# Block 0 of a fused attention and two-MLP kernel: one weight-decoding turn a step, with GpSimd's share and the attention's pieces put elsewhere in the step

## The chip, the cores and the metric

The kernel runs on one core of one Trainium2 chip. Five engines have a queue each and run it strictly in order: TensorE (PE, matmuls), VectorE (DVE), ScalarE (ACT), GpSimd (POOL) and SyncE (SP, which here only starts DMAs). They wait for each other through semaphores. The metric is the device time of one execution in microseconds (us); less is better.

## The reference, cut to what matters

```python
q_s = softmax(q over features)           # q, k, v: 8 batches, 8 heads, 576 rows, 64 features, float32
k_s = softmax(k over the sequence)
x = q_s @ (k_s^T @ v)                    # per batch and head; then (4608 tokens, 512)
h = x @ moe_w_in                         # 512 -> 2048; the weights come as 8-byte floats
x = (h - tanh(h)) @ moe_w_out            # 2048 -> 512
h = x @ moe2_w_in                        # 512 -> 2048
out = (P(h) / (Q(h) + 1e-6)) @ moe2_w_out    # P a cubic, Q = 1 + |b0||h| + |b1|h^2
```

## The kernel before, in words

The 4608 tokens are nine blocks j of 512. In the first MLP a step n treats one slice f = n % 16 of 128 hidden features of block j = n // 16. A float32 operand is split into a rounded high part and the low rest, and each product is three matmuls (`mm3`, lines 80 to 82): so `first_product(f)` is 12 matmuls of 128x512 into `hps`, and `second_product1` of the step two before (LAG1 = 2) is 12 more into `acc`. Between them stand, for every step: `t` = tanh(hps) on ACT (line 983), `hps` = hps - t on DVE (line 986, called sub here), `gh`, the high part, on ACT (line 336), and `gl`, the low part (line 340), on DVE in block 0 and on POOL later. `gh` and `gl` have two buffers, so a new `gh` waits until the second product of two steps before has read the old one.

Steps 0 to 15 are block 0, and only there the weights of the first MLP are still on their way: each 128x512 piece arrives as 8-byte floats (`raw`, 512 KB, three buffers) and is decoded. ACT makes two pieces of the word (`e` line 131, `m` line 133); DVE takes the sign (`and`, line 134), shifts (line 146) and adds (line 147); ACT copies the high part (`wa..h`, `wb..h`, line 154, called high here); DVE or POOL takes the low part (`wa..l`, `wb..l`, line 158, called low). 32 pieces are needed in block 0, seven of which are opened in the prologue. One call of `decode` opens one piece, joins (shift and add) the one opened in the call before, and takes the high and the low part of still older ones. Block 0 has two such calls in a step (one in steps 2 and 6): the first between sub and `gl`, with its low on DVE, the second behind `gl`, with its low on POOL.

Beside that, block 0 prepares the attention of block 1, in pairs of heads p = 0 to 3 that begin every third step: `kv_max` (DVE, lines 456 and 457), `kv_turn` (PE), `kv_top` (DVE, `mc`, line 474), `kv_back` (PE, line 479, needs `mc`), `kv_sub` (DVE, `ke`, line 485), `kv_exp` (ACT, line 495), `kv_mm` (PE) and `kv_norm` (`rs` on DVE, `bd` on ACT, line 527); and for the queries `q_max` (DVE, `qm`), `q_sub` (POOL), `q_exp` (ACT, line 605), `q_sum` (`qs` in three DVE instructions from line 610, then a multiplication on POOL, line 613), `q_turn` and `q_mm` (PE), `q_copy` and `q_out` (ACT, `qh` and four copies to `xr`, line 674). `work[n]` lists what step n does of it; `front` issues the plain entries at the head of the step, `turn` the PE half of the paired ones, and `follow` their second half, behind `gl`.

The order on every engine is the order in which this program is written. From step 16 on there is no decoding of this kind and no part of the change.

Of the kernel before, what the change touches and what calls it, by code (L numbers as in the profile page):

```python
# [18 lines left out]
P = 128  # L19
# [24 lines left out]
def attention_moe_moe2_kernel(ctx, tc, q, k, v, w1, w2, w3, w4, ca, cb, out):  # L44
# [31 lines left out]
    def f32(ap):  # L76
        return ap.bitcast(F32)
# [24 lines left out]
        [(0, "a", 0)] + [x for f in range(-1, KF) for x in ((0, "b", f), (0, "a", f + 2)) if 0 <= x[2] < KF],  # L102
        [(1, w, f + i) for f in range(0, KF, 2) for w in "ab" for i in range(2)],
    ]
    staged, joining, parting = [], [], []

    def staging():
        return rawp.tile([P, 2 * NB], F32, tag="raw", name="raw")
# [14 lines left out]
    def dec_open(t):  # L123


        words = t.bitcast(U32).rearrange("p (n two) -> p n two", two=2)
        e = decp.tile([P, NB], F32, tag="e", name="e", bufs=3)
        m = decp.tile([P, NB], U32, tag="m", name="m", bufs=4)


        ACT.activation(out=e, in_=f32(words[:, :, 1]), func=AF.Copy, scale=2.0**-112)
        halves = m.bitcast(U16).rearrange("p (n two) -> p n two", two=2)
        ACT.activation(out=halves[:, :, 0], in_=words[:, :, 0], func=AF.Copy, scale=2.0**-29)
        DVE.tensor_scalar(  # L134
            out=halves[:, :, 1],
            in0=t.bitcast(U16).rearrange("p (n four) -> p n four", four=4)[:, :, 3],
            scalar1=0x8000,
            scalar2=None,
            op0=ALU.bitwise_and,
        )  # L140
        return e, m
# [18 lines left out]
    def dec_start():  # L160

        old = [joining.pop()] if joining else []
        if staged:
            piece, t = staged.pop(0)
            if wide:
                joining.append((piece, t, *dec_open(t)))
            else:
                old.append((piece, t, None, t))
        return old

    def dec_end(ph, old, low_on_dve):
        if parting and parting[0][2]:
            dec_low(*parting.pop(0)[:2], low_on_dve)
        for x in parting:
            dec_high(*x[:2])
            x[2] = True
        if wide:
            for _, _, e, m in old:
                dec_join(e, m)
        parting.extend([piece, m, False] for piece, _, _, m in old)  # L180
        fetch_w(ph)

    def decode(ph, low_on_dve):
        dec_end(ph, dec_start(), low_on_dve)

    parked = {}
    UNITS = (1, 5, 2, 6, 7, 4, 3)
# [495 lines left out]
    def front(todo):  # L685
        for fn, args in todo:
            if not isinstance(fn, tuple):
                fn(*args)

    def turn(todo):  # L690

        got = []
        for fn, args in todo:
            if isinstance(fn, tuple):
                fn[0](*args)
                got.append(lambda fn=fn, args=args: fn[1](*args))
        return got

    def follow(after):
        for fn in [late for fn in after for late in [fn()] if late]:  # L700
            fn()

# [19 lines left out]
    for j in range(1, NBLK):  # L722
        for p in range(NPAIR):
            if j < B:
                s, at = kv_from[j, p], kv_at[j, p]
                steps = (s - 2, s - 1 - (p == 0), s - (p == 0), s + (p > 0), at) if j == 1 else (s - 3, s - 3, s - 1, s, s, s, at)
                for fn, s in zip(KV if j == 1 else KV_LATER, steps):
                    if fn is not kv_max or (j, p) != (1, 0):
                        put(s, fn, j, p)
            s, at = q_from[j, p], q_at[j, p]  # L730
            steps = (s - 1, s, s + 1, s + 2, at - 2, at) if j == 1 else (s - 1, s, s + 1, s + 2, s + 3, s + 5, at)
            for fn, s in zip(Q if j == 1 else Q_LATER, steps):
                if fn is not q_max or (j, p) != (1, 0):
                    put(s, fn, j, p)
        for p in range(2, NPAIR + 2):
            to, before = (j + p // NPAIR, p % NPAIR), (j + (p - 2) // NPAIR, (p - 2) % NPAIR)
            if to in kv_at:
                put(kv_from[before] + 1, load_k, *to)
                put(kv_at[before] + 1, load_v, *to)
            if to in q_at:  # L740
                put(q_from[before] + 2, load_q, *to)

    with tc.manual_schedule():
# [21 lines left out]
        for s in range(NPAIR + 4):  # L765
            def at(k, *fns):

                return [fn(0, s - k) for fn in fns if 0 <= s - k < NPAIR]

            at(1, kv_turn)  # L770
            at(2, kv_back)
            at(3, kv_mm, q_turn)
            at(4, q_mm)
            at(0, kv_max, q_max, q_sub)
            at(1, q_exp)
            at(1, kv_top)
            at(2, q_sum)
            at(2, kv_sub, kv_exp)
            at(3, kv_sum, q_copy)
            at(3, kv_parts)  # L780
            if s < NPAIR + 3:
                if s >= 2:
                    decode(0, False)
                at(5, q_out)
            else:
                kv_max(1, 0)
                q_max(1, 0)
                at(5, q_out)
                at(4, q_out)
                decode(0, False)  # L790
                decode(0, False)
# [150 lines left out]

        STEPS = NBLK * KF
        PAIRS = STEPS // 2
        due = {}
        last = STEPS - KF
        for n in range(STEPS):
            j, f = n // KF, n % KF
            leave = None
            front(work[n])  # L950
            flush()
            hps = first_product(f)
            if f == KF - 1 and j + 1 < NBLK:
                next_x()
            if n == last:
                ACT.activation(out=absb, in_=coef[:, 4:6], func=AF.Abs)
                DVE.tensor_scalar(out=coef[:, 0:4], in0=coef[:, 0:4], scalar1=-1.0, scalar2=None, op0=ALU.mult)
            if n == last + 10:
                for errand in todo:
                    for _ in errand:  # L960
                        flush()
                flush()
                for pool in (att, bdp, decp, rawp):
                    pool.release()
                outp = ctx.enter_context(tc.tile_pool(name="outp", bufs=4, side="right"))
                rp = ctx.enter_context(tc.tile_pool(name="rp", bufs=2, side="right"))
                xup = ctx.enter_context(tc.tile_pool(name="xup", bufs=1, side="right"))
                units = [xup.tile([P, NB], F32R, tag=f"u{k}", name=f"u{k}") for k in range(12)]
                units += [w[:, c, :] for w in (xh, xl) for c in range(KC)]
# [5 lines left out]
            if n in due:  # L975
# [5 lines left out]
            after = turn(work[n])  # L981
            t = gp.tile([P, NB], F32, tag="t", name="t", bufs=1)
            ACT.activation(out=t, in_=hps, func=AF.Tanh)  # L983

            g = t if j else hps
            DVE.tensor_tensor(out=g, in0=hps, in1=t, op=ALU.subtract)  # L986
            ph_w, turns = None, 0
            if j == 0:
                ph_w, turns = 0, 1 if f in (2, 6) else 2
            gh, gl = split_high(g)  # L990
            due[n + LAG1] = lambda a=(j, f, gh, gl): second_product1(*a)
            if turns:
                decode(ph_w, True)
            split_low(g, gh, gl, POOL if j else DVE)
            follow(after)
            if leave:
                leave()
            if turns > 1:
                decode(ph_w, False)
            if n == KF:  # L1000
                fetch_w(1)
            if n > KF:
                for errand in todo:
                    next(errand, None)
            if n == STEPS - 1:

                ACT.activation(out=ahead, in_=bias_q, func=AF.Abs_reciprocal_sqrt)
# [69 lines left out]
```

## Time and profile before

| | |
|---|---|
| time, three runs | 1654.87 us median (1653.03 to 1655.1) |
| the profiled execution | 1656.78 us, span 1655.0 us |
| PE busy | 1615.7 us, 98% of the span |
| DVE, ACT, POOL busy | 67%, 62%, 63% of the span |
| step 1's sub to step 13's, in block 0 | 79.83 us, 12 steps |

A share over the whole span says little of block 0, which is one sixteenth of it and the only stretch in which DVE is nearly full. Times in rows are microseconds from the span's start, and a row's second number is how long the instruction took. The distance between two starts on one engine is often a little shorter than that, since an instruction begins before the last one has left the engine; the sums go by these distances.

### The profile page before, as it was taken

Reading aid. Unit: us, or ns where it says so; the run is one execution under the profiler, and the core shown is the slowest. Engines: PE = TensorE matmul, PEld = TensorE weight load, DVE = VectorE, ACT = ScalarE, POOL = GpSimd, SP = SyncE. Lnnn points to the kernel's source line nnn. Section 1 sums busy time; section 2 is a strip of 40 time slices with the busy share of each in tenths; the row PEclk is TensorE's granted clock in tenths of the full one; section 3 lists DMA queues with packets and bytes.
Section 4 is the critical chain, followed back from the end, with each engine's and each line's share of the span. In section 5 each row is a group of like instructions: output and inputs, shape, how many; then the busy total and the mean of one; then the engine's idle time right before and its main releaser. Section 6 shows DMA issues by size and latency. Waiting matters only on the chain.

```text
span 1655.0 us, 26931 instructions
## 1 busy us (share of the span) xinstructions
PE 1615.7 (98%) x9400; PEld 1375.3 (83%) x9400; DVE 1109.6 (67%) x1839; ACT 1024.5 (62%) x1821; POOL 1039.2 (63%) x876
## 2 busy tenths in 40 slices
PE   5999999999999999999999999999999999999998
PEld 3777888888888888887888989898999999999996
DVE  7997656575565556351214787778787777878786
ACT  6785554544545455443326777777777777777775
POOL 4223727374554637373435888888888877888775
PEclk9999999999999999999999999999999999999999
DMA  8662766666474756351487575858585757676640
GB/s 233 192 182 80 217 175 191 169 186 190 147 208 118 227 150 202 104 174 56 142 305 284 178 281 193 285 189 295 190 297 199 276 195 265 206 252 217 208 139 26
DMA packets 250729, 323.76 MB, mean 196 GB/s; under 512 B 119008, under 2 KB 185568, under 8 KB 241376
## 3 DMA queue, kind: packets, MB, share of 16 engines
q1 hardware_dynamic: 250592, 322.03, 60.9%
q8 instruction: 74, 1.21, 0.3%
q14 instruction: 63, 0.52, 0.1%
HBM read 249.04 MB, written 72.93 MB: 195 GB/s over the span
## 4 chain that ended last, share of the span: by engine, by line
PE 82%; DVE 7%; DMA 3%; ACT 3%; issue 2%; SPq 1%; POOL 1%; DVEq 0%; ACTq 0%; POOLq 0%
PE acc L80 14%; PE acc L81 14%; PE acc L82 14%; PE z L871 12%; PE y L871 9%; PE hps L80 6%; PE hps L81 6%; PE hps L82 6%; DVE m L147 1%; DVE m L134 1%; PE kvps L515 1%; PE xps L660 1%; DMA xh<-x2d 1%; DVE e L146 1%; DVE xl L322 0%
## 5 line engine op out<-in xcount | busy, mean ns | idle before, releaser
L340 POOL TENSOR_TENSOR gl<-t,gh 128x512 fp32r<-128x512 f32 x128 | 174.1, 1360 | 301.0 <-ACT gh L336 278.1
L928 POOL TENSOR_TENSOR n<-n,r 128x512 f32<-128x512 f32 x144 | 186.6, 1296 | 98.2 <-ACT r L925 93.0
L986 DVE TENSOR_TENSOR t<-hps,t 128x512 f32<-128x512 f32 x128 | 88.1, 688 | 233.4 <-ACT t L983 233.4
L336 ACT CAST gh<-t 128x512 fp32r<-128x512 f32 x128 | 79.8, 623 | 248.0 <-PE acc L82 140.5
L928 POOL TENSOR_TENSOR n<-n,n 128x512 f32<-128x512 f32 x144 | 186.7, 1296 | 36.1 <-ACT n L912 36.1
L928 POOL TENSOR_TENSOR n<-n,h 128x512 f32<-128x512 f32 x144 | 187.2, 1300 | 9.7 <-DMA xl<-x2d 9.6
L983 ACT ACTIVATE t<-hps 128x512 f32<-128x512 f32 x144 | 86.0, 597 | 121.0 <-PE hps L82 85.3
L882 ACT COPY sums<-z 128x256 f32<-128x256 f32 x144 | 53.8, 374 | 135.0 <-PE z L871 135.0
L908 ACT ACTIVATE n<-h,coef 128x512 f32<-128x512 f32 x144 | 116.7, 810 | 0.3 <-POOL n L928 0.3
L938 DVE CAST gh<-a 128x512 fp32r<-128x512 f32 x144 | 99.6, 692 | 16.5 <-PE z L871 0.9
L941 DVE TENSOR_TENSOR gl<-a,gh 128x512 fp32r<-128x512 f32 x144 | 99.7, 692 | 15.2 <-DVE gh L938 0.5
L934 DVE SCALAR_TENSOR_TENSOR a<-a,n 128x512 f32<-128x512 f32 x144 | 100.0, 695 | 14.3 <-POOL n L928 8.5
L917 DVE SCALAR_TENSOR_TENSOR a<-h,absb,a 128x512 f32<-128x512 f32 x144 | 107.6, 747 | 3.0 <-ACT a L902 2.9
L902 ACT ACTIVATE a<-h,coef 128x512 f32<-128x512 f32 x144 | 100.5, 698 | 2.7 <-DVE gl L941 2.7
L931 DVE SCALAR_TENSOR_TENSOR a<-a,r 128x512 f32<-128x512 f32 x144 | 99.4, 690 | 0.8 <-ACT r L925 0.8
L920 ACT ACTIVATE r<-a,bias_q 128x512 f32<-128x512 f32 x144 | 97.3, 676 | 0.0
L925 ACT ACTIVATE r<-r 128x512 f32<-128x512 f32 x144 | 91.2, 634 | 4.6
L905 ACT ACTIVATE h<-h 128x512 f32<-128x512 f32 x144 | 89.3, 620 | 0.9 <-DMA xh<-x2d 0.8
L889 DVE TENSOR_TENSOR h<-y,sums 128x256 f32<-128x256 f32 x72 | 30.6, 425 | 58.6 <-PE y L871 58.6
L893 DVE TENSOR_TENSOR h<-y,top 128x512 f32<-128x512 f32 x72 | 49.7, 691 | 27.4 <-ACT top L882 27.1
L613 POOL TENSOR_TENSOR qe<-qe,qs 128x512 f32<-128x512 f32 x36 | 40.6, 1128 | 38.7 <-DVE qs L612 35.4
L80 PE MATMUL acc<-wb3h,gh 128*128 128x512 f32 x144 | 57.0, 396 | 2.9 <-DVE gh L938 2.9
(296 smaller groups left out, 5114.2 us busy)
## 6 DMA issues: line engine op xcount, KB each, us to landing
u<-x2d SPq DMA_DIRECT2D x78, 256.0 KB, 5.5
raw<-in_moe_w_in_dram SPq DMA_DIRECT2D x32, 512.0 KB, 4.8
raw<-in_moe_w_out_dram SPq DMA_DIRECT2D x32, 512.0 KB, 4.1
x2d<-raw SPq DMA_DIRECT2D x64, 256.0 KB, 3.5
x2d<-xr SPq DMA_DIRECT2D x56, 256.0 KB, 3.8
wa0h<-wa0d SPq DMA_DIRECT2D x9, 1024.0 KB, 5.0
wa1h<-wa2d SPq DMA_DIRECT2D x9, 1024.0 KB, 5.0
wa2h<-wa4d SPq DMA_DIRECT2D x9, 1024.0 KB, 5.2
```

The costliest lines, as they stand in the source:

```text
L80: PE.matmul(o, lhi, rhi, start=start, stop=False)
L81: PE.matmul(o, lhi, rlo, start=False, stop=False)
L82: PE.matmul(o, llo, rhi, start=False, stop=stop)
L340: eng.tensor_tensor(out=gl, in0=g, in1=f32(gh), op=ALU.subtract)
L871: PE.matmul(o, w, x[:, xc], start=m in (1, 5) and c == k == 0, stop=c == 1 and k == 2, skip_group_check=True,)
L902: ACT.activation(out=new(t, "a", ps_a), in_=t["h"], func=AF.Abs, scale=b0)
L908: ACT.activation(out=new(t, "n1"), in_=t["h"], func=AF.Identity, scale=a3, bias=a2)
L917: DVE.scalar_tensor_tensor(out=t["a"], in0=t["h2"], scalar=b1, in1=t["a"], op0=ALU.mult, op1=ALU.add)
L928: return lambda t: POOL.tensor_tensor(out=t[a], in0=t[a], in1=t[b], op=op)
L934: DVE.scalar_tensor_tensor(out=t["a"], in0=t["a"], scalar=2.0, in1=t["n0"], op0=ALU.subtract, op1=ALU.mult)
L938: DVE.tensor_copy(out=t["g"][0], in_=t["a"])
L941: DVE.tensor_tensor(out=t["g"][1], in0=t["a"], in1=f32(t["g"][0]), op=ALU.subtract)
```

## The change

It gives block 0 one turn a step in place of two calls. A step opens two pieces, joins the same two in the same step, and takes the high part of the first of them at its end (`highs(1)`) and of the second at the head of the next step, right behind tanh (`highs(2)`). POOL's low part is issued there too; DVE's low part comes behind `gl`. The plain attention entries named in `BESIDE` move from the head of a step to the place between sub and `gl`; `kv_exp` and `q_exp` (`CLOSING`) move to the step's end; `kv_top` and `kv_sub` (`beside`) run between sub and `gl` of the next step instead of behind `gl` of their own. The prologue joins one piece more and fetches one more. One load of keys is a step later. All 32 pieces and all arithmetic stay.

```diff
+    def opens(n):
+        for _ in range(min(n, len(staged))):
+            piece, t = staged.pop(0)
+            if wide:
+                opened.append((piece, *dec_open(t)))
...
+            fetch_w(0)
+    def joins(n):
+        for _ in range(min(n, len(opened))):
+            piece, e, m = opened.pop(0)
+            if wide:
                 dec_join(e, m)
+            joined.append((piece, m))
+    def highs(n):
+        for _ in range(min(n, len(joined))):
+            dec_high(*joined[0])
+            ready.append(joined.pop(0))
+    def lows(*engines):
+        for eng in engines[:len(ready)]:
+            dec_low(*ready.pop(0), eng is DVE)
...
+    BESIDE = (kv_max, kv_squares, kv_join, kv_sub, q_max, q_sub, q_sum, q_squares)
+    CLOSING = (kv_exp, q_exp)
...
-            front(work[n])
+            front(work[n], () if j else BESIDE + CLOSING)
...
             ACT.activation(out=t, in_=hps, func=AF.Tanh)
             g = t if j else hps
             DVE.tensor_tensor(out=g, in0=hps, in1=t, op=ALU.subtract)
-            ph_w, turns = None, 0
-            if j == 0:
-                ph_w, turns = 0, 1 if f in (2, 6) else 2
+            if not j:
+                highs(2)
+                first = ready[0:1]
+                del ready[0:1]
+                lows(POOL, POOL)
+                follow(beside)
+                only(work[n], BESIDE)
+                if n in due:
+                    due.pop(n)()
+                after = turn(work[n])
+                beside = [x for x in after if x[0] in (kv_top, kv_sub)]
+                after = [x for x in after if x not in beside]
             gh, gl = split_high(g)
             due[n + LAG1] = lambda a=(j, f, gh, gl): second_product1(*a)
-            if turns:
-                decode(ph_w, True)
             split_low(g, gh, gl, POOL if j else DVE)
+            if not j:
+                for x in first:
+                    dec_low(*x, True)
+                opens(2)
+                joins(2)
+                highs(1)
             follow(after)
+            if not j:
+                only(work[n], CLOSING)
             if leave:
                 leave()
-            if turns > 1:
-                decode(ph_w, False)
```

On ACT, at the end of step 2, the kernel before has these rows, from step 2's `gh` to the next tanh (`t`). `m` and `e` open a piece, `wa1h` and `wb0h` are highs, `ke` and `qe` the two exponentials.

```order
L336 CAST gh<-hps 128x512
L131 ACTIVATE e<-raw 128x512
L133 ACTIVATE m<-raw 128x512
L154 CAST wa1h<-m 128x512
L131 ACTIVATE e<-raw 128x512
L133 ACTIVATE m<-raw 128x512
L154 CAST wb0h<-m 128x512
L495 ACTIVATE ke<-ke 128x640
L605 ACTIVATE qe<-qe 128x512
L983 ACTIVATE t<-hps 128x512
```

The changed kernel has, for the same stretch and on to the next step's first rows:

```order
L344 CAST gh<-hps 128x512
L131 ACTIVATE e<-raw 128x512
L133 ACTIVATE m<-raw 128x512
L131 ACTIVATE e<-raw 128x512
L133 ACTIVATE m<-raw 128x512
L154 CAST wa1h<-m 128x512
L503 ACTIVATE ke<-ke 128x640
L613 ACTIVATE qe<-qe 128x512
L1001 ACTIVATE t<-hps 128x512
L154 CAST wb1h<-m 128x512
```

Before, a high copied a piece that had been joined one call earlier; now `wa1h` copies the piece whose `e` and `m` stand three and four rows above it, and the exponentials and the tanh are queued behind it.

On DVE, the kernel before has these rows from step 2's sub to step 3's: `gl` is the low part of g, `wb0l` a decoding low, and `qs` and `mx` are the attention's of step 3's head.

```order
L986 TENSOR_TENSOR hps<-hps,t 128x512
L134 TENSOR_SCALAR m<-raw 128x512
L158 TENSOR_TENSOR wb0l<-m,wb0h 128x512
L146 TENSOR_SCALAR e<-e 128x512
L147 ISA m<-e,m 128x1024
L340 TENSOR_TENSOR gl<-hps,gh 128x512
L610 TENSOR_REDUCE qs<-qe 128x8
L611 TENSOR_SCALAR qs<-qs 128x8
L612 RECIPROCAL qs<-qs 128x8
L456 TENSOR_TENSOR mx<-kt_159 128x256
L457 TENSOR_TENSOR mx<-mx,kt_159 128x128
L986 TENSOR_TENSOR hps<-hps,t 128x512
```

And the changed kernel's step 3, which has the same attention entries, from its sub to its second shift (an add and step 4's sub follow):

```order
L1004 TENSOR_TENSOR hps<-hps,t 128x512
L618 TENSOR_REDUCE qs<-qe 128x8
L619 TENSOR_SCALAR qs<-qs 128x8
L620 RECIPROCAL qs<-qs 128x8
L464 TENSOR_TENSOR mx<-kt_159 128x256
L465 TENSOR_TENSOR mx<-mx,kt_159 128x128
L348 TENSOR_TENSOR gl<-hps,gh 128x512
L158 TENSOR_TENSOR wa1l<-m,wa1h 128x512
L134 TENSOR_SCALAR m<-raw 128x512 x2
L146 TENSOR_SCALAR e<-e 128x512
L147 ISA m<-e,m 128x1024
L146 TENSOR_SCALAR e<-e 128x512
```

The decoding left the place between sub and `gl`, the attention went there, and the whole turn stands behind `gl`.

On DVE at the start of block 0, the kernel before has `mc` (for `kv_back` of step 1) behind step 0's `gl`:

```order
L147 ISA m<-e,m 128x1024
L340 TENSOR_TENSOR gl<-hps,gh 128x512
L474 TENSOR_REDUCE mc<-kvps 128x1
L134 TENSOR_SCALAR m<-raw 128x512
L146 TENSOR_SCALAR e<-e 128x512
```

The changed kernel has it behind step 1's sub, with step 0's whole turn in between:

```order
L348 TENSOR_TENSOR gl<-hps,gh 128x512
L158 TENSOR_TENSOR wb0l<-m,wb0h 128x512
L134 TENSOR_SCALAR m<-raw 128x512 x2
L146 TENSOR_SCALAR e<-e 128x512
L147 ISA m<-e,m 128x1024
L146 TENSOR_SCALAR e<-e 128x512
L147 ISA m<-e,m 128x1024
L1004 TENSOR_TENSOR hps<-hps,t 128x512
L482 TENSOR_REDUCE mc<-kvps 128x1
```

PE's own order is the same in both kernels: first product of the step, second product of two steps before, then the attention's matmuls.

## Rows read from the trace of the kernel before

**Rows 1.** Stretches: us, busy of PE, PEld, DVE, ACT, POOL; clock; DMA share, GB/s.

```profile
47.94:127.77 79.83, 77.88 (x448) 60.86 (x447) 74.74 (x141) 60.94 (x113) 20.52 (x17) 0.99 0.59 178
127.77:148.01 20.24, 16.62 (x76) 12.38 (x74) 15.91 (x29) 11.94 (x25) 4.00 (x4) 0.92 0.16 38
```

**Rows 2.** Instruction groups, DVE, the first of these stretches: busy us, mean ns.

```profile
L134 DVE TENSOR_SCALAR m<-raw 128x512 uint16<-128x512 uint16 x22 | 15.7, 712 | 0.0
L146 DVE TENSOR_SCALAR e<-e 128x512 uint32<-128x512 uint32 x22 | 10.8, 493 | 0.0
```

**Rows 3.** Timeline of DVE, steps 2 and 3: start, duration, instruction.

```profile
54.37 0.70 DVE L986 TENSOR_TENSOR hps<-hps,t 128x512 f32<-128x512 f32 x1
54.98 0.46 DVE L134 TENSOR_SCALAR m<-raw 128x512 uint16<-128x512 uint16 x1
55.32 0.67 DVE L158 TENSOR_TENSOR wb0l<-m,wb0h 128x512 fp32r<-128x512 f32 x1
55.92 0.42 DVE L146 TENSOR_SCALAR e<-e 128x512 uint32<-128x512 uint32 x1
56.37 0.69 DVE L147 CUSTOM_DVE_ANT_0 m<-e,m 128x1024 uint16<-128x1024 uint16 x1
56.98 0.68 DVE L340 TENSOR_TENSOR gl<-hps,gh 128x512 fp32r<-128x512 f32 x1
57.58 0.68 DVE L610 TENSOR_REDUCE qs<-qe 128x8 f32<-128x512 f32 x1
...
58.61 0.37 DVE L456 TENSOR_TENSOR mx<-kt 128x256 f32<-128x256 f32 x1
59.02 1.02 DVE L457 TENSOR_TENSOR mx<-mx,kt 128x128 f32<-128x128 f32 x1
```

**Rows 4.** Timelines of POOL and DVE: instructions beside each other, and one alone.

```profile
58.84 1.05 POOL L613 TENSOR_TENSOR qe<-qe,qs 128x512 f32<-128x512 f32 x1 [6.47 <-DVE qs L612]
...
80.34 0.29 DVE L457 TENSOR_TENSOR mx<-mx,kt 128x128 f32<-128x128 f32 x1
...
51.06 1.31 POOL L158 TENSOR_TENSOR wa1l<-m,wa1h 128x512 fp32r<-128x512 f32 x1 [4.15 <-ACT wa1h L154]
...
51.14 0.81 DVE L485 TENSOR_TENSOR ke<-kt,kvps 128x640 f32<-128x640 f32 x1
```

**Rows 5.** Timeline of ACT: exponentials, tanh and gh of step 2; step 7's copies.

```profile
52.61 0.73 ACT L495 ACTIVATE ke<-ke 128x640 f32<-128x640 f32 x1
53.24 0.61 ACT L605 ACTIVATE qe<-qe 128x512 f32<-128x512 f32 x1
53.77 0.57 ACT L983 ACTIVATE t<-hps 128x512 f32<-128x512 f32 x1
55.16 0.59 ACT L336 CAST gh<-hps 128x512 fp32r<-128x512 f32 x1 [0.82 <-DVE hps L986]
...
87.67 1.52 ACT L674 COPY xr<-xps 64x256 f32<-64x256 f32 x4
89.21 0.32 ACT L527 ACTIVATE bd<-xps,rs 128x64 f32<-128x64 f32 x1
```

**Rows 6.** Timelines of DVE and ACT: an add and its high; a gh and its gl.

```profile
39.23 0.69 DVE L147 CUSTOM_DVE_ANT_0 m<-e,m 128x1024 uint16<-128x1024 uint16 x1
...
39.96 0.62 ACT L154 CAST wb0h<-m 128x512 fp32r<-128x512 f32 x1 [1.49 <-DVE m L147]
...
136.59 0.59 ACT L336 CAST gh<-hps 128x512 fp32r<-128x512 f32 x1 [2.99 <-DVE hps L986]
...
137.21 0.69 DVE L340 TENSOR_TENSOR gl<-hps,gh 128x512 fp32r<-128x512 f32 x1
```

**Rows 7.** Timeline of PE: kv_back of step 1; step 14's second product, and the next.

```profile
45.03 0.32 PE L479 MATMUL kvps<-identity,mc 128*128 128x128 f32 x1 [3.47 <-DVE mc L474]
...
145.27 0.40 PE L80 MATMUL acc<-gh,wb3h 128*128 128x512 f32 x1
...
148.01 0.39 PE L80 MATMUL hps<-xh,wa0h 128*128 128x512 f32 x1
```

More of the change, by code (lines that the diff above doesn't have):

```diff
@@ L104, in attention_moe_moe2_kernel @@
     ]
-    staged, joining, parting = [], [], []
+    staged, opened, joined, ready = [], [], [], []
     def staging():
@@ L158, in dec_low, with decode @@
         (DVE if on_dve else POOL).tensor_tensor(out=lo, in0=f32(m), in1=f32(hi), op=ALU.subtract)
-    def dec_start():
-        old = [joining.pop()] if joining else []
-        if staged:
+    def opens(n):
+        for _ in range(min(n, len(staged))):
             piece, t = staged.pop(0)
             if wide:
-                joining.append((piece, t, *dec_open(t)))
+                opened.append((piece, *dec_open(t)))
             else:
[L168 to L178, printed above, removed]
-                dec_join(e, m)
[L180 to L184, printed above, removed]
+                m = decp.tile([P, NB], U32, tag="m", name="m", bufs=4)
+                POOL.tensor_copy(out=f32(m), in_=t)
+                opened.append((piece, None, m))
+            fetch_w(0)
[3 more added lines that the diff above has]
+            if wide:
+                dec_join(e, m)
+            joined.append((piece, m))
[6 more added lines that the diff above has]
+            dec_low(*ready.pop(0), eng is DVE)
+    def decode():
+        n, r = len(opened), len(ready)
+        opens(1)
+        lows(*[POOL] * r)
+        highs(1)
+        joins(n)
     parked = {}
@@ L683, in attention_moe_moe2_kernel, with front, only @@
     Q_LATER = (q_max, q_sub, q_exp, q_sum, q_squares, q_fetch, (q_mm, q_out))
-    def front(todo):
+    BESIDE = (kv_max, kv_squares, kv_join, kv_sub, q_max, q_sub, q_sum, q_squares)
+    CLOSING = (kv_exp, q_exp)
+    def front(todo, leave=()):
         for fn, args in todo:
-            if not isinstance(fn, tuple):
+            if not isinstance(fn, tuple) and fn not in leave:
+                fn(*args)
+    def only(todo, these):
+        for fn, args in todo:
+            if fn in these:
                 fn(*args)
@@ L695, in turn @@
                 fn[0](*args)
-                got.append(lambda fn=fn, args=args: fn[1](*args))
+                got.append((fn[1], args))
         return got
     def follow(after):
-        for fn in [late for fn in after for late in [fn()] if late]:
-            fn()
+        for fn, args in after:
+            fn(*args)
     work = {s: [] for s in range(NBLK * KF)}
@@ L737, in attention_moe_moe2_kernel @@
             if to in kv_at:
-                put(kv_from[before] + 1, load_k, *to)
+                put(kv_from[before] + (2 if before[0] == 1 else 1), load_k, *to)
                 put(kv_at[before] + 1, load_v, *to)
@@ L782, in attention_moe_moe2_kernel @@
                 if s >= 2:
-                    decode(0, False)
+                    decode()
                 at(5, q_out)
@@ L789, in attention_moe_moe2_kernel @@
                 at(4, q_out)
-                decode(0, False)
-                decode(0, False)
+                decode()
+                decode()
+                joins(1)
+                fetch_w(0)
             if s in (4, 5):
@@ L944, in attention_moe_moe2_kernel @@
         PAIRS = STEPS // 2
-        due = {}
+        due, beside = {}, []
         last = STEPS - KF
@@ L974, in attention_moe_moe2_kernel @@
                     load_unit(0, u)
-            if n in due:
+            if j and n in due:
                 leave = due.pop(n)()
@@ L980, in attention_moe_moe2_kernel @@
                 ring(f // 4 - 1)
-            after = turn(work[n])
+            after = turn(work[n]) if j else []
             t = gp.tile([P, NB], F32, tag="t", name="t", bufs=1)
@@ L986, in attention_moe_moe2_kernel @@
             DVE.tensor_tensor(out=g, in0=hps, in1=t, op=ALU.subtract)
-            ph_w, turns = None, 0
-            if j == 0:
-                ph_w, turns = 0, 1 if f in (2, 6) else 2
+            if not j:
[10 more added lines that the diff above has]
+                after = [x for x in after if x not in beside]
             gh, gl = split_high(g)
             due[n + LAG1] = lambda a=(j, f, gh, gl): second_product1(*a)
-            if turns:
-                decode(ph_w, True)
             split_low(g, gh, gl, POOL if j else DVE)
+            if not j:
[3 more added lines that the diff above has]
+                joins(2)
+                highs(1)
             follow(after)
+            if not j:
+                only(work[n], CLOSING)
             if leave:
                 leave()
-            if turns > 1:
-                decode(ph_w, False)
             if n == KF:
```

## The prediction

> **What bounds the kernel now.** I read the shares of the engines first (PE 98% of the span), so anything that delays PE costs its full length and anything else costs nothing. Then the waits of PE inside block 0, since the change touches nothing else, and the busy times of the engines in two stretches: step 1's sub to step 13's, and from there to the second first product of block 1, at 148.01 us [rows 1, 7]. In the first, 79.83 us for twelve steps (6.65 us each), PE is busy for 77.88 and DVE for 74.74: both are nearly full, and only 1.95 us of PE is idle. In the second, 20.24 us, PE is busy for 16.62 and its granted clock is 0.92. Ahead of both lies one wait of 3.47 us, when `kv_back` of step 1 stands on PE for `mc` from DVE [rows 7]. So a shorter DVE step could win little more than PE's idle time, while a step that becomes longer than 6.65 us by DVE or ACT is paid almost in full.
>
> Second, I read DVE's and ACT's timelines for what a step is made of. DVE's starts follow each other by 0.61 us (sub), 0.34 (and), 0.60 (low), 0.45 (shift), 0.61 (add) and 0.60 (gl) [rows 3]. Part of DVE's time is stretching: the and takes 0.712 us on average and 0.46 where nothing is beside it, the shift 0.493 and 0.42 [rows 2, 3], in all 22 x 0.25 + 22 x 0.07 = 7.1 us. The last row of the DVE timeline shows what stretches: the second `kv_max` instruction took 1.02 us beside a POOL multiplication that ran from 58.84 to 59.89, and 0.29 alone [rows 3, 4].
>
> **The change: removed.** The stretching of ands and shifts. POOL's low starts when its high is done, now right behind tanh, and lies beside sub, attention and `gl`; the ands come later. `ke` took 0.81 us beside a POOL low of 1.31 and so wasn't held until that ended [rows 4]; the ones that read PSUM or one tensor I cost at nothing. So up to 7.1 us of DVE's work goes.
>
> **Added: a circle of waits.** This decides. Before, a high on ACT copied a piece joined a call earlier, so tanh of the next step didn't wait for this step's DVE work. Now the last high of a step waits for the first add of the same step, and tanh of the next step is queued behind it on ACT; sub waits for tanh, `gh` for sub, `gl` for `gh`, and the low, the ands, the shift and that add stand behind `gl` on DVE. A step can't be shorter than once around: tanh to sub 0.60, sub to gh 0.79 [rows 3, 5], gh to gl 0.62 [rows 6], gl 0.60, low 0.60, two ands 0.68, shift 0.45 [rows 3], add to high 0.73 [rows 6], high to tanh 0.53 (as exponential to tanh) [rows 5]: **5.60 us**, in which DVE stands idle for 0.80 between sub and gl (0.79 + 0.62 - 0.61). The rest of the second piece's work hides beside high and tanh. Twelve steps: 67.2, less 0.3 as step 12 has one piece only: 66.9.
>
> **Added: what lies on the circle besides.** *On ACT, between high and tanh*, nothing hides the closing entries: `kv_exp` 0.63 in steps 2, 6, 9, 12; `q_exp` 0.53 in step 2; `q_copy` about 0.53 in 5, 8, 11, 12; in steps 7 and 10 four copies, `bd` and `q_exp`, 1.54 + 0.22 + 0.53 = 2.29 [rows 5]; in step 4 `bd` waits for `rs`, which DVE takes behind its second add, about 0.8 + 0.22 + 0.53 = 1.56. Sum: 2.5 + 0.5 + 2.1 + 4.6 + 1.6 = **11.3 us**. *On DVE, between sub and gl*, the attention is free only up to the 0.80. `qs` takes 1.03 (57.58 to 58.61), the maxima 0.41 + 0.29, `ke` 0.8, and `qm` and `mc` I take as 0.6 and 0.4 by the like rows [rows 3, 4]. Over 0.80: steps 2 (ke, qm) 0.6, 3 (qs, maxima) 0.9, 5 and 8 (mc, qs, qm) 1.2 each, 6 and 9 (ke, maxima) 0.7 each, 11 (mc, qs) 0.6: **5.8 us** with rounding.
>
> **Added: two-input instructions beside POOL.** POOL's low now runs from about 1.2 to 2.5 us behind tanh, and `q_sub` or `q_sum`'s product follows it at once (1.05) [rows 4]. The maxima stand in that place: the first waits for the low (0.5), the second for POOL's next (1.0). Steps 6 and 9: 1.55 each; step 3: 1.3: **4.4 us**. Bounds: nothing, or this. I take it whole because the row of 1.02 us is the same instruction. DVE's own low also reads two SBUF tensors and meets `q_sub` or the product in steps 1 (1.1), 3 (0.5) and 11 (0.7): **2.3 us**. No row shows this pair; bounds nothing and 2.3, and I take the upper, by its likeness to that row. The Trainium skill (SBUF — State Buffer, Who interferes with whom) says that a VectorE instruction with two SBUF inputs contends with a GpSimd instruction that reads SBUF, and that the later one blocks fully: by it the 2.3 is paid, without it the sum would be 2.3 less. The trace agrees for the maxima (1.02 against 0.29); for the low no row tells.
>
> **Moved: `mc` and `kv_back`.** `mc` of step 1 now stands behind step 0's whole turn and step 1's tanh and sub. The prologue's extra join puts sub of step 0 off by 1.06, to 42.4; once around from there (0.79 + 0.62 + 0.60 + 0.60 + 0.68 + 0.45 + 0.73 + 0.53 + 0.60, and 0.4 for a low behind POOL's) is 6.0, so sub of step 1 comes at 48.4 (before 47.94): **+0.5**. PE's wait for `mc` grows from 3.47 to about 8 us (45.03 to 49.4). It is not on the circle, but the product behind it is late and may run at a lower clock, and `gh` of step 2 waits for the second product of step 0 behind that: **+0.8** (bounds 0 and 2). The loads issued by SP keep three raw buffers and are needed a whole step after their issue; the later load of keys has two steps: nothing. Should these covers fail, a step waits by what a load is late.
>
> **Moved: the end of the turns.** Pieces are all opened by step 12, before by step 13. From tanh of step 13 on PE has only its own work: `kv_mm` (about 1.3 until its end), six halves of a step at 2.74 (145.27 to 148.01 for twelve matmuls [rows 7]) and 1.0 for `q_mm`: 18.8, or 18.2 from sub, against 20.24 [rows 1]: **-2.0**.
>
> **Sum.** 66.9 + 11.3 + 5.8 + 4.4 + 2.3 + 0.8 = 91.5 for the twelve steps, against 79.83: +11.7; with +0.5 and -2.0: **+10.2 us**. The profiled execution took 1656.78 (its span 1655.0), so 1667.0 by its own time; it lies 1.9 above the median of the runs, and the forecast for a median is 1654.87 + 10.2 = 1665. From block 1 on nothing changes and PE is full, so nothing is given back.
>
> **The rivals.** *DVE's relief wins (faster).* If ACT's closing entries and the attention overlap so well that a step falls under 6.65 us, that is, if what is added to the 5.60 stays under 1.05 us a step (I count 2.05), DVE's saved 7.1 us would count until PE is full: at most 1.95 in the first stretch and 2.0 in the second: -3.9, 1651. For it speaks that ACT is busy for only 60.94 of 79.83 us; against it, that ACT's queue is in order and its idle time lies in front of the entries that wait. The same section of the Trainium skill would have it that a VectorE instruction with at most one SBUF input, outside its two-port modes, doesn't meet GpSimd at all, which is what the new place for POOL's low uses. *The meetings with POOL cost nothing (no change).* Without 4.4, 2.3 and 0.8 the sum is +2.7: 1657.6. *PE's clock (slower still).* PE would be busy for 77.9 of 91.5 us, 85%, near the 82% of the second stretch, whose clock was 0.92 [rows 1]. If PE at a lower clock makes `gh` wait in several steps, 2 us for each of two or three: 1670.
>
> **Chances.** Forecast (1660 to 1669) 0.58; nothing from POOL 0.17; faster 0.12; PE's clock 0.10; else 0.03. The range that leaves out no more than 2 in 10 is 1654 to 1669. A measurement of this kernel can tell about 0.2%, 3.3 us, from no change. Faster by more than that 0.12, within 0.18, slower 0.70.
>
> **What would show it.** In the changed kernel, twelve steps from step 1's sub to step 13's should take about 91 us; ACT should wait for DVE's add ahead of the high at each step's end, and DVE for tanh ahead of sub, most in steps 2, 4, 7, 10; ands and shifts should take about 0.46 and 0.42; the maxima of steps 3, 6 and 9 about 1 us each; `kv_back` of step 1 should wait for some 8 us; PE should idle by 1 to 2 us a step. I am wrong if tanh doesn't wait behind that high, or if DVE stays busy through the place between sub and gl.

## The result, and the profile after

The changed kernel takes 1663.0 us (median of 4 runs, 1661.59 to 1664.41), the kernel before 1654.47 us on the same chip: ratio 1.0053, 95% interval 1.0035 to 1.007. Forecast: 1665 us, slower. The profiled execution took 1661.59 us, its span is 1659.8.

The same two stretches as in [rows 1], for the changed kernel: from step 1's sub to step 13's, and on to the second first product of block 1.

```profile
47.53:138.40 90.87, 80.62 (x428) 63.47 (x430) 72.39 (x140) 65.26 (x117) 24.10 (x20) 0.92 0.51 158
138.40:156.26 17.86, 17.86 (x109) 14.32 (x105) 15.71 (x27) 9.21 (x20) 1.88 (x2) 1.00 0.21 51
```

The twelve steps take 90.87 us instead of 79.83, the stretch behind them 17.86 instead of 20.24, and block 1's second first product starts at 156.26 instead of 148.01: 8.25 us later, near the 8.5 us by which the medians differ. The whole spans of the two traces differ by only 4.8 us (1659.8 and 1655.0): behind that point, where all kernels here run the same program, the changed kernel's trace is 3.5 us shorter. Single executions scatter there, from 1502.6 us (e1 below) to 1508.2 (e4). So the medians and ratios tell how long a kernel takes, and a trace tells where in block 0 time goes.

DVE is busy for less (72.39, was 74.74) and yet the steps are longer, so it waits. For what, the view of waits says (engine, what waited, what for; us in total, times, longest), from 40 to 155 us of the changed kernel:

```profile
DVE hps L1004 <- ACT t L1001: 11.3, 11, 2.3
PE kvps L487 <- DVE mc L482: 11.1, 4, 8.0
...
ACT wa3h L154 <- DVE m L147: 7.0, 4, 2.4
ACT wa1h L154 <- DVE m L147: 6.5, 4, 3.0
...
ACT wa2h L154 <- DVE m L147: 5.0, 4, 1.9
...
DVE gl L348 <- ACT gh L344: 4.5, 7, 0.7
```

In the kernel before, sub waited for tanh for 1.2 us in all:

```profile
DVE hps L986 <- ACT t L983: 1.2, 2, 0.8
```

Now DVE waits for tanh and, in the same steps, ACT waits for DVE's add: two engines waiting for each other in turn. One turn of it stands in the timelines of step 2 (start, duration, instruction, idle time ahead of it and what ended it). DVE:

```profile
54.19 0.70 DVE L1004 TENSOR_TENSOR hps<-hps,t 128x512 f32<-128x512 f32 x1
...
56.92 0.69 DVE L348 TENSOR_TENSOR gl<-hps,gh 128x512 fp32r<-128x512 f32 x1 [0.72 <-ACT gh L344]
57.53 0.68 DVE L158 TENSOR_TENSOR wa1l<-m,wa1h 128x512 fp32r<-128x512 f32 x1
58.13 0.80 DVE L134 TENSOR_SCALAR m<-raw 128x512 uint16<-128x512 uint16 x2
58.82 0.42 DVE L146 TENSOR_SCALAR e<-e 128x512 uint32<-128x512 uint32 x1
59.37 0.69 DVE L147 CUSTOM_DVE_ANT_0 m<-e,m 128x1024 uint16<-128x1024 uint16 x1
...
62.40 0.70 DVE L1004 TENSOR_TENSOR hps<-hps,t 128x512 f32<-128x512 f32 x1 [1.16 <-ACT t L1001]
```

And ACT, in the same step:

```profile
56.30 0.59 ACT L344 CAST gh<-hps 128x512 fp32r<-128x512 f32 x1 [1.56 <-PE acc L82]
...
60.10 0.62 ACT L154 CAST wa1h<-m 128x512 fp32r<-128x512 f32 x1 [0.76 <-DVE m L147]
60.62 0.73 ACT L503 ACTIVATE ke<-ke 128x640 f32<-128x640 f32 x1
61.26 0.61 ACT L613 ACTIVATE qe<-qe 128x512 f32<-128x512 f32 x1
61.78 0.58 ACT L1001 ACTIVATE t<-hps 128x512 f32<-128x512 f32 x1
```

The reader goes round it: sub 54.19, `gh` 56.30, `gl` 56.92, low 57.53, ands 58.13, shift 58.82, add 59.37, high 60.10, the two exponentials that nothing hides, tanh 61.78, and the next sub at 62.40. That `gh` starts 2.11 us behind sub and not 0.79 is PE's second product, the forecast's term for step 2.

The time is PE's in the end: over the steps it is busy for 80.62 us where it was 77.88, at a granted clock of 0.92 instead of 0.99, and idle for 10.25 instead of 1.95. 2.74 + 8.30 are the 11.04 us. The matmuls are not quite the same ones (428 records for 448), since some of a step's work moves across the stretch's end.

### The profile page after: what moved, and what is told of

It is laid out like the page before. It is cut to its first block, busy times and chain, and to the rows that moved or that the text cites. A ratio compares the mean times of both kernels' runs of the same rounds, so it can differ in the third digit from the quotient of the medians.

```text
span 1659.8 us, 26916 instructions
## 1 busy us (share of the span) xinstructions
PE 1614.9 (97%) x9400; PEld 1376.0 (83%) x9400; DVE 1104.3 (67%) x1838; ACT 1026.4 (62%) x1821; POOL 1041.0 (63%) x877
## 4 chain that ended last, share of the span: by engine, by line
PE 88%; DVE 4%; DMA 3%; ACT 3%; SPq 1%; issue 1%; POOL 0%; DVEq 0%; ACTq 0%; POOLq 0%
PE acc L80 15%; PE acc L81 15%; PE acc L82 14%; PE z L889 12%; PE y L889 9%; PE hps L80 7%; PE hps L81 7%; PE hps L82 7%; DMA xh<-x2d 1%; PE xps L668 1%; PE kvps L523 1%; DMA u<-x2d 1%; DVE m L147 1%; ACT m L133 0%; DMA qd<-qt 0%
## 5 line engine op out<-in xcount | busy, mean ns | idle before, releaser
L926 ACT ACTIVATE n<-h,coef 128x512 f32<-128x512 f32 x144 | 116.6, 810 | 0.3 <-POOL n L946 0.3
L930 ACT ACTIVATE n<-h,coef 128x512 f32<-128x512 f32 x72 | 58.1, 806 | 2.5 <-DVE a L952 2.5
```

The lines of the kernel that those rows point to most:

```text
L926: ACT.activation(out=new(t, "n1"), in_=t["h"], func=AF.Identity, scale=a3, bias=a2)
```

## The experiments

Each kernel ran beside the kernel before on the same chip; the ratio is to that. "Steps" is step 1's sub to step 13's, "block 1" the start of its second first product, both from one profiled execution each. The two traces of the changed kernel differ by 0.23 us in the steps and by 1.46 in block 1, so smaller differences in these columns tell nothing.

| kernel | median us | ratio, 95% interval | steps | block 1 |
|---|---|---|---|---|
| before | 1652.3 to 1654.5 | 1 | 79.83 | 148.01 |
| changed | 1663.0 | 1.0053, 1.0035 to 1.007 | 90.87 | 156.26 |
| changed, again (a1) | 1663.39 | 1.0058, 1.0045 to 1.007 | 91.10 | 157.72 |
| e1, last high in the next step | 1658.63 | 1.0046, 1.0032 to 1.0059 | 84.94 | 152.77 |
| e2, maxima at the head | 1662.72 | 1.0061, 1.0047 to 1.0074 | 88.62 | 155.41 |
| e3, closing entries ahead of the high | 1661.43 | 1.0057, 1.0044 to 1.007 | 87.88 | 155.56 |
| e4, the circle put into before | 1672.4 | 1.0118, 1.0104 to 1.0132 | 92.49 | 162.98 |
| e9, `mc` in its own step | 1663.27 | 1.0051, 1.0035 to 1.0066 | 90.93 | 156.67 |
| e11 = e1 + e9 | 1657.72 | 1.0028, 1.0019 to 1.0038 | 85.09 | 151.21 |
| e5 = e1 + `rs` behind `gl` | 1657.98 | 1.0033, 1.0021 to 1.0046 | 86.21 | 154.99 |
| e6 = e5 + maxima at the head, low behind sub | 1658.19 | 1.0029, 1.0017 to 1.0042 | 84.38 | 152.90 |
| e7 = e6 + `mc` of step 0 in its step | 1658.98 | 1.0032, 1.0021 to 1.0044 | 83.53 | 153.34 |
| e8 = e7 + each `mc` and the copies behind `gl` | 1651.32 | 0.9982, 0.9973 to 0.9991 | 79.66 | 145.36 |
| e10 = e8 + `ke` behind `gl` | 1651.56 | 0.9984, 0.9974 to 0.9993 | 79.77 | 144.47 |

The changed kernel again, beside the later runs:

> The changed kernel once more, as the measure of the others beside it. Both theories: 8 to 9 us over the kernel before (ratio 1.0053), step 1's sub to step 13's about 90.9 us.

The theory is that of the prediction: the high at a step's end closes a circle of waits over DVE and ACT, and what else stands on it adds up. The main rival is that DVE's meetings with POOL, not the circle, make the steps long.

**The circle itself: e1 takes the high out, e4 puts it into the kernel before.** e1:

```diff
                 joins(2)
-                highs(1)
```

> The changed kernel without the last high of a step: both pieces' highs are taken at the head of the next step, behind tanh. Theory (circle of waits): tanh no longer waits for the same step's add, so DVE's own work sets the step: 4.61 us of decoding and product work, the place between sub and gl at 0.95 or the attention in it, and the meetings with POOL, together about 80 us from step 1's sub to step 13's (changed kernel 90.9, before 79.8), the start and the tail as in the changed kernel: 1652 to 1655 us. DVE no longer waits for tanh. Rival (the meetings of two-input DVE instructions with POOL are the cause): they stay, even grow since POOL's low starts later, so at least 7 of the 11 us stay: 1660 us or more.

The twelve steps lose 5.93 us, block 1 comes 3.5 us earlier. 2.3 of the 5.93 lie in step 12 alone (4.20 us for 6.50), and the stretch behind it is 2.1 longer (19.96 for 17.86), so the 3.5 of 8.25 us at block 1 is the fairer size: less than half of the loss. The expected 80 us and 1652 to 1655 were missed; 1658.63 is nearer to the rival's 1660, and the ratio, 1.0046, can't be told from the changed kernel's. In e1, sub waits for tanh in four places only (5.4 us), and three of them, 1.44, 1.39 and 1.39 us, are the ends of steps 4, 7 and 10. ACT there, at the end of step 4:

```profile
75.30 0.31 ACT L535 ACTIVATE bd<-xps,rs 128x64 f32<-128x64 f32 x1 [2.24 <-DVE rs L529]
75.51 0.62 ACT L613 ACTIVATE qe<-qe 128x512 f32<-128x512 f32 x1
76.03 0.59 ACT L1001 ACTIVATE t<-hps 128x512 f32<-128x512 f32 x1
```

`rs` stands behind the second add on DVE, and `bd` ahead of tanh on ACT: a second way round, which the prediction had in its term for step 4 and this expectation left out.

e4, in `decode` of the kernel before, which joins first and takes the high of the piece just joined:

```diff
-        for x in parting:
-            dec_high(*x[:2])
-            x[2] = True
         if wide:
             for _, _, e, m in old:
                 dec_join(e, m)
         parting.extend([piece, m, False] for piece, _, _, m in old)
+        for x in parting:
+            if not x[2]:
+                dec_high(*x[:2])
+                x[2] = True
```

> The kernel before with one thing of the change alone: a call of decode joins first and takes the high of the very piece that it has joined, so tanh of the next step is queued behind a high that waits for this step's last add. Nothing else is moved; the attention and POOL's low stay where they were. Theory: once around is sub, and, low, shift, add, gl, and, shift, add, high, tanh, sub = 5.9 us, and kv_top, kv_sub (4 us over the block), ACT's closing entries (11 us) and stretching (5 us) lie on it: about 91 us from step 1's sub to step 13's: 1662 to 1668 us. Rival (the new places of the attention and of POOL's low are the cause): as before, 1655 us.

The edit does a little more than put the changed kernel's wait in: both calls of a step now have such a high, the last of them stands behind the step's second add (the changed kernel's behind its first), and a piece's low comes one call earlier, so it can fall to the other engine. The attention and the turns stay where they were. The twelve steps take 92.49 us, about as long as in the changed kernel. The view of waits of e4:

```profile
DVE hps L987 <- ACT t L984: 13.0, 10, 1.8
```

So such waits are enough for a loss of this kind, without the new places of the attention and of POOL's low. The sizes can't be set side by side: e4's circle is longer, its step 1 comes 4.0 us late already (sub at 51.92 for 47.94), and its 1672.4 us lie above the 1662 to 1668 that were expected.

**Two sizes: e2 and e3.** e2 takes `kv_max` out of `BESIDE`, so the maxima stand at the step's head again; e3 moves `only(work[n], CLOSING)` ahead of `highs(1)`.

> The changed kernel with kv_max issued at the head of a step again, ahead of sub, where DVE waits for tanh. Theory: steps 3, 6 and 9 become shorter by what the maxima now take between sub and gl, 0.9 to 1.8 us each, about 4 us in all: 1659 us, and the maxima take 0.37 and 0.29 us again. Rival (meetings with POOL carry the whole loss): 1655 us or less. Rival (they cost nothing, since DVE isn't what the step waits for): 1663 us.

> The changed kernel with kv_exp and q_exp ahead of the last high of the step, where ACT waits for DVE's add (0.8 to 3.0 us), in place of behind it. Theory: steps 2, 6, 9 and 12 become shorter by about 0.65 us each and steps 4, 7 and 10 by 0.5: about 4 us in all, 1659 us; the other copies (q_copy, xr, bd) stay behind the high. Rival (ACT's entries are hidden anyway): 1663 us.

e2 shortens the steps by 2.25 us, e3 by 2.99, both in the direction of the theory and both less than 4. Of that, block 1 sees 0.85 and 0.70, less than two traces of one kernel differ by, and the ratios don't differ from the changed kernel's: neither is resolved in the time. The circle is left in both.

**PE's long wait ahead of `kv_back`: e9.**

```diff
-                beside = [x for x in after if x[0] in (kv_top, kv_sub)]
+                beside = [x for x in after if x[0] is kv_sub]
...
             if not j:
+                follow([x for x in after if x[0] is kv_top])
+                after = [x for x in after if x[0] is not kv_top]
                 for x in first:
```

> The changed kernel with one part undone: mc right behind gl of its own step; the high at the step's end stays, and so the circle. Circle theory: PE's waits ahead of kv_back (11.1 us in four places, 8.0 of them in step 1) go or fall to 3 to 4, but the steps are paced by the circle, mc adds 0.4 to it in four steps, and the time stays within 1.5 us of the changed kernel. Rival, late mc and kv_back pace the steps: the time falls by 5 to 8 us, to that of the kernel before.

The largest single idle time of PE in the changed kernel, 8.04 us, falls to 3.38, and the time stays (1.0051 beside 1.0053 and 1.0058). PE's waits only change their names; e9's longest are

```profile
PE xps L523 <- ACT ke L503: 6.4, 2, 4.0
PE kvps L487 <- ACT bd L535: 3.6, 1, 3.6
PE kvps L487 <- DVE mc L482: 3.4, 1, 3.4
```

PE can't do the steps' work before the circle gives it `gh` and `gl`; where it stands meanwhile is of no account. 

> The changed kernel with two parts undone, the high at the step's end and the late mc, and nothing else moved: maxima, low and rs stay where the change put them. The first alone gave 3.5 us at the second first product of block 1, the second alone nothing. Theory, the two waits cover each other: with both gone PE no longer waits for mc and the step is free to be PE's, so they give together more than one by one, 6 to 8 us, to within 0 to 3 us over the kernel before; what is left are tanh's three waits of 1.4 us behind rs in steps 4, 7 and 10 and the maxima beside POOL. Rival, rs behind the second add still closes the circle in steps 4, 7 and 10, and the maxima and the low stretch, so that DVE and ACT set the pace: no more than the high alone, 5 to 7 us over the kernel before, and rs, maxima and low were needed for the gain.

e11 has both edits. Steps 85.09 us, as in e1: `rs` still holds tanh (three waits). By the medians it is 3.8 us over the kernel before, between the theory (0 to 3) and the rival (5 to 7). Block 1 comes 1.6 us earlier than in e1, but single traces scatter by as much, and the intervals of the two ratios overlap: that the edit of e9 is worth more with the circle open is not shown by this run.

**To a better kernel, part by part: e5 to e8, e10.** e5, on top of e1:

```diff
             if not j:
+                follow([x for x in after if x[0] is kv_norm])
+                after = [x for x in after if x[0] is not kv_norm]
                 for x in first:
```

> The changed kernel without the high at the step's end, and with rs of the keys' sums taken right behind gl, ahead of the step's decoding. Circle theory: without that high, the circle was still closed in steps 4, 7 and 10 by rs, which stood behind the second add and held bd, q_exp and tanh on ACT (three waits of sub for tanh, 1.39 to 1.44 us, in the run without the high alone, where the twelve steps took 84.94 us). With rs early these three waits go: the twelve steps take 80 to 81 us, the start of the second first product of block 1 comes at 149 to 150 us, and the whole is 1 to 3 us over the kernel before. Rival, the attention's place and its meetings with POOL pace the step: the waits for tanh turn into other waits of DVE or are taken up by stretched instructions, twelve steps 84 to 85 us as before, 4 to 6 us over the kernel before.

The number was missed: 86.21 us. Sub's wait for tanh at the end of step 4 is down to 0.21 us, at the end of steps 7 and 10 it is 1.9 us instead of 1.4. e7, which has the same order there, shows why on ACT, in step 7:

```profile
92.62 0.32 ACT L535 ACTIVATE bd<-xps,rs 128x64 f32<-128x64 f32 x1 [1.17 <-DVE rs L529]
92.84 0.66 ACT L131 ACTIVATE e<-raw 128x512 f32<-128x512 f32 x1
...
95.23 1.49 ACT L682 COPY xr<-xps 64x256 f32<-64x256 f32 x4
96.74 0.63 ACT L613 ACTIVATE qe<-qe 128x512 f32<-128x512 f32 x1
97.40 0.60 ACT L1001 ACTIVATE t<-hps 128x512 f32<-128x512 f32 x1
```

ACT waits for `rs` with nothing ahead of it to do, and then the openings of two pieces (four instructions), four copies and an exponential, 4.78 us from `bd` to tanh, are all in front of tanh.

e6 and e7, each on top of the one before (`kv_max` out of `BESIDE` as in e2):

```diff
             DVE.tensor_tensor(out=g, in0=hps, in1=t, op=ALU.subtract)
             if not j:
                 highs(2)
                 first = ready[0:1]
                 del ready[0:1]
+                for x in first:
+                    dec_low(*x, True)
...
             if not j:
-                for x in first:
-                    dec_low(*x, True)
+                if not n:
+                    follow(beside)
+                    beside = []
                 follow([x for x in after if x[0] is kv_norm])
```

> As the run with rs behind gl, and in addition the maxima of the keys at the head of the step, and DVE's decoding low right behind sub in place of behind gl. Theory: the maxima fall back to 0.4 and 0.3 us, the low fills the gap that DVE has between sub and gl, so DVE's step falls by about 1 us in the steps that have maxima and by 0.6 in the others, and PE (77.9 us of work in twelve steps) sets the pace: twelve steps 78 to 79 us, second first product of block 1 at 146 to 147 us, the whole 1 to 3 us under the kernel before. Rival, the low beside POOL's low stretches to 1.3 to 1.6 us and puts gl off by as much as it saves: twelve steps 81 us or more and no gain over the run with rs behind gl alone.

> As the run with rs, maxima and low moved, and in addition mc of step 0's keys right behind step 0's gl, as in the kernel before. Theory: PE's wait ahead of kv_back of step 1 falls from 8.0 us to 3 to 4; with PE setting the pace this is taken off the end nearly whole: second first product of block 1 at 142 to 145 us, the whole 4 to 6 us under the kernel before. Rival, that wait stands beside the circle and the twelve steps' pace is DVE's: the start of the twelve steps moves, their end does not, and the time is that of the run without this edit within 1 us.

Both were expected to be faster than the kernel before, and neither is. e6 takes 1.83 us from the steps, and its ratio can't be told from e5's. e7 is its rival's case: the first wait of `kv_back` falls from 8.39 to 3.69 us, and the second grows from 2.52 to 4.31.

e8 puts all of a step's second halves directly behind `gl`, ahead of the openings:

```diff
-                beside = [x for x in after if x[0] in (kv_top, kv_sub)]
+                beside = [x for x in after if x[0] is kv_sub]
...
-                if not n:
-                    follow(beside)
-                    beside = []
-                follow([x for x in after if x[0] is kv_norm])
-                after = [x for x in after if x[0] is not kv_norm]
+                follow(after)
                 opens(2)
                 joins(2)
-            follow(after)
+            else:
+                follow(after)
```

This moves more than its expectation names: besides `mc`, ACT's copies (`qh`, and `xr` ahead of `bd`) come in front of the openings.

> As the run with rs, maxima, low and first mc moved, and in addition every mc right behind gl of its own step, as in the kernel before. In that run PE idled for 4.31, 1.39 and 2.69 us ahead of kv_back of steps 4, 7 and 10, where mc stood behind the next step's sub; and the next tanh waited for PE's first product (9.1 us in all). Theory: with these three waits gone PE is the pace; the three waits (8.4 us) come off the end nearly whole, the second first product of block 1 starts at 145 to 148 us, and the whole is 0 to 3 us under the kernel before. Rival, those idles only mark time that PE would have had to wait anyway for gl and sub, because DVE's and ACT's step is as long: twelve steps stay at 83 to 84 us, the whole 4 to 5 us over the kernel before.

Block 1 comes 7.98 us earlier than in e7, and the kernel is faster than before: ratio 0.9982, interval 0.9973 to 0.9991. The same place on ACT as above:

```profile
90.90 1.51 ACT L682 COPY xr<-xps 64x256 f32<-64x256 f32 x4
92.44 0.31 ACT L535 ACTIVATE bd<-xps,rs 128x64 f32<-128x64 f32 x1
...
95.57 0.58 ACT L1001 ACTIVATE t<-hps 128x512 f32<-128x512 f32 x1
```

The copies fill the time in which ACT waited for `rs`; tanh comes 3.13 us behind `bd`, and the next sub waits for 0.26 us instead of 1.93. PE's waits for `mc` of steps 4, 7 and 10 are gone too. Which of the two moves gave how much was not tried apart, nor whether e8 still needs the earlier moves of e6.

> As the run with every mc in its own step, and in addition the keys' subtraction ke behind gl of its own step too, so that nothing is left of the change but the opening and joining of two pieces a step, POOL's low right behind tanh and the queries' entries between sub and gl. Theory: ke then delays the step's decoding by 0.8 us in four steps, where DVE has room by now (its work of about 73 us in twelve steps of 79 to 80), and ke's exponential no longer comes late for the product behind it: within 1 us of the run with mc alone moved. Rival, ke pushes the second add and with it the next step's sub back: 2 to 3 us longer than that run.

e10 is level with e8 (0.9984 and 0.9982, intervals over each other).

Where e8's gain over the kernel before is shows in one stretch, from 43 us to block 1's second first product, in the kernel before, the changed one and e8 (columns as in [rows 1]):

```profile
43.00:148.01 105.01, 97.41 (x531) 75.58 (x531) 95.42 (x175) 76.44 (x145) 26.98 (x23) 0.97 0.51 153
```

```profile
43.00:156.26 113.26, 98.48 (x531) 77.79 (x531) 92.34 (x175) 77.84 (x143) 26.95 (x23) 0.92 0.46 139
```

```profile
43.00:145.36 102.36, 94.38 (x530) 75.12 (x531) 93.32 (x178) 78.38 (x145) 32.03 (x24) 0.98 0.51 157
```

The changed kernel's 8.25 us over the kernel before are 1.07 us of longer busy time for as many matmuls (531 records) and 7.18 of idle time (14.78 less 7.60). e8 is idle for nearly as long as the kernel before (7.98 us) and is busy for 3.03 us less with the same matmuls: 2.65 us in all, in one trace each, where the medians differ by 2.3.

## Why the prediction was right, point by point

- **The circle of waits** carried the forecast. The waits stand in the trace, e4 shows that such a circle costs this much (+12.66 us of steps, with a longer circle), and e1 that the late high is part of the loss (-3.5 of 8.25 us at block 1). That the circle is all of it is not shown: e1 keeps 4.8 us, three waits behind `rs` are 4.2 us of its steps, and it took the moves of e8 together to win the rest. Its pieces, from the rows of step 2 above: `gh` to `gl` 0.62, `gl` 0.61, low 0.60, ands 0.69, add to high 0.73, tanh to sub 0.62, each within 0.02 of the forecast. Only shift to add was 0.55 for 0.45, some 0.1 us a step or 1.2 in all.
- **Step by step**, the forecast's terms against the distances of subs in the trace:

| step | 1 | 2 | 3 | 4 | 5 | 6 | 7 | 8 | 9 | 10 | 11 | 12 |
|---|---|---|---|---|---|---|---|---|---|---|---|---|
| forecast | 6.7 | 8.2 | 8.3 | 7.2 | 7.3 | 8.5 | 7.9 | 7.3 | 8.5 | 7.9 | 7.4 | 6.5 |
| measured | 6.66 | 8.21 | 7.93 | 7.42 | 7.36 | 8.03 | 8.01 | 7.38 | 8.02 | 8.00 | 7.35 | 6.50 |

  Nine of twelve agree within 0.3 us; the sum is 91.5 and 90.87 (the rounded entries add up to 91.7, and the forecast's 5.8 for the attention is 5.9 by its own entries). That the sums are so near is partly luck: the 1.2 us missing between shift and add make up for about half of what the meetings with POOL were over-sized by.
- **The meetings with POOL** were over-sized. Steps 3, 6 and 9 are the three that come out 0.4 to 0.5 short. The maxima were stretched as forecast (1.02 us), but from the first of them to `gl` step 3 takes 1.35 us and step 6 1.76, against 0.70 alone: 2.8 us with step 9 instead of 4.4, and e2's 2.25 fits that. The lows, for which no row of before told, cost 0.90, 0.25 and 0.58 in steps 1, 3 and 11 (1.58, 0.93 and 1.26 us, against 0.68 elsewhere): 1.7 for 2.3. So the price was nearer to the upper bound.
- **The relief of ands and shifts** came as forecast: 18.8 us for 23 of each, where 22 of each took 26.5, so 7.7 us against "up to 7.1". It made no step shorter than before, because the circle's waits took more than it gave. It isn't worthless: the ands and the first shift stand on the circle, whose 5.60 us were reckoned with their short lengths. The groups of DVE over the twelve steps (busy us, mean ns; [rows 2] before):

```profile
L146 DVE TENSOR_SCALAR e<-e 128x512 uint32<-128x512 uint32 x23 | 9.6, 416 | 0.0
L134 DVE TENSOR_SCALAR m<-raw 128x512 uint16<-128x512 uint16 x23 | 9.2, 453 | 0.0
```

- **`mc` and `kv_back`**: forecast 8 us of PE's wait, measured 8.04; that it isn't on the circle is shown by e9. The start (+0.5 us) was -0.4 in the first trace and +0.8 in the second: sub of step 0 comes at 41.53 and 42.70, while step 0 itself takes the 6.0 us of the forecast in both. The tail was -2.4 for -2.0.
- **PE idle by 1 to 2 us a step** was too high: 0.85. The forecast's 77.9 us of work became 80.62, at a clock of 0.92 instead of 0.99. The rival of a lower clock wanted `gh` to wait for PE in several steps. It did so in steps 2 (1.56 us) and 6 (1.15), and only in step 2 did `gl` stand for it (0.72 us), for which the forecast had 0.8. So the slower matmuls lie inside the delay and not on top of it: the steps' sum from DVE and ACT alone held.

## What to carry to other kernels

Where several in-order queues share a loop, go round it: follow from an instruction to what it waits for until the next step's same instruction comes, and add the distances of starts; an engine that is busy for 80% can still wait in every step. A wait inside such a circle is paid in every step; a wait outside it, even PE's longest, can cost nothing while the circle is closed (8.04 to 3.38 us ahead of `kv_back`: no change of the time). When one is opened, look for the next: here `rs`, `mc` and the copies came to light behind the high, and only a kernel with several moves together (e8) was faster than before. Which of them were needed was not tried apart.

## What the hardware showed that I had not expected

- DVE's low beside POOL. It was a bound without a row; now there is one, DVE and then POOL in the changed kernel:

```profile
49.49 1.58 DVE L158 TENSOR_TENSOR wa1l<-m,wa1h 128x512 fp32r<-128x512 f32 x1
```

```profile
49.49 1.04 POOL L603 TENSOR_TENSOR qe<-qr,qm 128x512 f32<-128x512 f32 x1
```

  The low ends 0.54 us behind POOL's instruction, so nearly all of its 0.68 us ran after it. The Trainium skill (SBUF — State Buffer, Who interferes with whom) has a VectorE instruction with two SBUF inputs contend with a GpSimd instruction that reads SBUF; the trace agrees, now for this pair too.
- What a pause of PE costs afterwards. In the changed kernel, two stretches of 10 us:

```profile
70.00:80.00 10.00, 6.00 (x25) 4.46 (x24) 7.45 (x18) 7.86 (x15) 2.59 (x3) 0.82 0.87 264
80.00:90.00 10.00, 10.00 (x39) 8.10 (x38) 9.19 (x17) 6.71 (x12) 3.51 (x3) 0.83 0.33 109
```

  PE idles for 4 us in the first, and in the second, though busy throughout, its granted clock is 0.83 on the mean: about a third of that time at the lower level, 1.2 GHz. The Trainium skill (TensorE: Matmul & The Clock Gate, Part 1: The HAM clock gate) has the reduced clock as the state that idleness brings back and activity ends, which these rows agree with. Before, the same stood at the block's end, 3.08 us idle and then a row at 0.83:

```profile
130.00:140.00 10.00, 6.92 (x42) 4.93 (x40) 6.81 (x12) 6.87 (x17) 3.84 (x3) 1.00 0.18 46
140.00:150.00 10.00, 9.46 (x33) 7.44 (x34) 8.83 (x15) 4.66 (x9) 1.39 (x2) 0.83 0.27 70
```

  e8 has no idle time of PE there: its rows from 110 to 160 us show 10.00 busy and clock 1.00. The twelve matmuls of block 1's first product show the price. Before, they start here, and the next product starts 4.95 us later, at 145.27 [rows 7]:

```profile
140.32 0.51 PE L80 MATMUL hps<-xh,wa0h 128*128 128x512 f32 x1 [1.27 <-ACT xh L320]
```

  In e8 the same twelve take 2.72 us (139.92 to 142.64). Less 0.22 us of waiting among them, that is about 2.0 of the 3.03 us by which e8 is busy for less; where the rest lies is open.
